# The third unit's MLP in one piece with seven products for its output, ahead of the last blocks of the first two units

## The chip, the cores and the metric

The kernel runs on one core of one Trainium2 chip. The metric is device time in microseconds (us) of a whole execution; before the change it is 658.83 us, the median of 3 runs (657.85 to 659.45).

A core has a matrix engine (TensorE, PE in the profile, with its weight loads listed apart as PEld), VectorE (DVE), ScalarE (ACT), GpSimd (POOL), and a queue (SP) that issues the transfers. Each works through its own list of instructions and waits for the others where it needs their results.

## The reference

A gated linear attention feeds an MLP. Sizes: 4 batches, 8 heads, 768 tokens, 48 channels per head; the MLP goes from 384 to 2048 and back.

```python
f = 1.0 / (1.0 + np.exp(-f_logit))
for t in range(S):
    state = f[:, :, t, :, None] * state + np.einsum('bhd,bhe->bhde', k[:, :, t], v[:, :, t])
    y[:, :, t] = np.einsum('bhd,bhde->bhe', q[:, :, t], state)
# (B,H,S,D) -> (B*S, H*D)
x = y.transpose(0, 2, 1, 3).reshape(B * S, H * D)
h = x @ w_in
g = h * (1.0 / (1.0 + np.exp(-1.702 * h)))
out = g @ w_out
```

Where the weights reach the kernel as 64-bit floats, it turns them into 32-bit ones itself ("conversions").

## The kernel before

The 3072 tokens are cut into 12 units of 256, numbered 0 to 11. A unit has an attention, written as a list of parts, and an MLP. The MLP of one unit fills TensorE while the attention of a later unit waits for the other engines. `merge` emits the parts of one unit's attention and, after each, a share of the list `fill`; each entry of the list has a width in columns, a function that emits it, and the number of converted weight pieces that it needs.

The MLP exists in two forms. For the first three units it is cut into four blocks of 4 x 128 hidden columns, as the weights arrive: `h` (48 products of 256 columns over the four blocks), then `o` with 32 products of 384 columns, summed up over the blocks in `sums`.

```python
def mlp_block(n, r):
    g, ffs = {}, range(r * FG, (r + 1) * FG)      # FG = 4, NGR = 4 blocks
    def done(tt, po):
        ...                                       # tile sums[n] at the first block
        acc = sums[n][:, tt]
        if r == 0:
            nc.scalar.copy(acc, po)
        else:
            nc.vector.tensor_tensor(acc, acc, po, ALU.add)
        if r == NGR - 1:
            store(n, tt, acc)
    return mlp_h(n, ffs, g), mlp_o(n, ffs, g, done)

def mlp_blocks(*blocks):                          # all h, then all o
    hs, os = zip(*(mlp_block(n, r) for n, r in blocks))
    return sum(hs, []) + sum(os, [])
```

From unit 3 on it is whole (`mlp_unit`), and `o` is made with seven products of half-sized matrices instead of eight: 56 products of 192 columns. These need sums of quarters of `w_out` (T, made once by `sums_of_b`) and sums of quarters of g (made per unit).

```python
def sums_of_b():
    for i in (1, 2, 3):
        T[i] = wp.tile(..., tag="bits", bufs=PAIRS_AHEAD)     # the place of the raw weights
    t4 = [wp.tile([P, DM], F32, tag="a", bufs=4) ...]
    for x in h: yield lambda x=x: sub(T[1][:, x], quarter(w_out, 0, 1, x), quarter(w_out, 0, 0, x))
    ...                                                       # T2, T3: two each; T4: four

def sums_of_a(n, g, b):
    j = b % 2
    if b < 2:
        g["S", j] = mlp.tile([P, FG, width(n)], F32, tag="g", bufs=6)
        tt(g["S", j][:, :, t1], g[j][:, :, t0], g[j][:, :, t1], ALU.subtract)
    else:
        tt(g[j][:, :, t1], g[j][:, :, t1], g[j + 2][:, :, t1], ALU.add)
        tt(g["S", j][:, :, t0], g[j][:, :, t1], g[j][:, :, t0], ALU.subtract)

def mlp_o7(n, g):
    ...
    products = (
        ("X", a(0, 0), b(0, 0), p1, True), ("W", a(1, 1), T_(4), p4, True), ("X", a(0, 1), b(1, 0), p2, False),
        ("Y", s(0), T_(2), p6, True), ("Z", a(1, 0), T_(1), p5, True), ("Y", s(1), T_(3), p7, False),
        ("Z", a(0, 1), b(1, 1), p3, False),
    )
    ...                                                       # 8 products of HC = 192 columns for each
    return [(HC, lambda p=p, f=f: one(*p, f), 0) for p in products for f in range(HF)]

def mlp_h(n, ffs, g, sums=False):
    def one(ff, c):
        if c == 0:
            if ff % FG == 0:
                g[ff // FG] = mlp.tile([P, FG, width(n)], F32, tag="g", bufs=6)
            t["ph"] = ps.tile([P, width(n)], F32, tag="mm", bufs=4)      # PSUM, shared with o
        nc.tensor.matmul(ph, lhsT=w_in[...], rhs=xTs[n][:, c, :], ...)
        if c == NK - 1:
            nc.scalar.activation(sg, ph, AF.Sigmoid, scale=1.702)
            nc.vector.tensor_tensor(g[ff // FG][:, ff % FG, :], ph, sg, ALU.mult)
            if sums and ff % FG == FG - 1:
                sums_of_a(n, g, ff // FG)
            ...
```

The conversions take five VectorE operations per piece of 128 x 384 (`chain`) and a copy on ScalarE; `convert()` emits one operation. The loop that mixes all this:

```python
def merge(n, fill, columns, share, pieces=0, hold=0, by=1.0, chores=()):
    parts = parts_of(n)
    ...
    for kind, fn in parts:
        ready = state["done"]                     # pieces converted so far
        fn()
        for chore in chores[:2]:
            chore()
        chores = chores[2:]
        at += share(kind)
        at_ops += converting.get(kind, 0)
        n_ops = min(int(pieces * NOP * at_ops / (by * total_ops)), pieces * NOP) - ops
        ...
        for i in range(n_ops):
            some(first + n_columns * i / n_ops)   # emit entries of fill up to this width
            convert()
        some(first + n_columns)
```

The parts of unit 3 are three score parts ("V"), a part that transposes the gates and queries of the next unit on VectorE, two that transpose keys on TensorE ("T"), one that transposes the next unit's keys on VectorE, and the state products ("S"). The calls:

```python
merge(0, fill, 0, steady, 8)
fill += mlp_blocks((0, 0)) + mlp_blocks((0, 1))
merge(1, fill, UNIT // 2 - LAG // 2, steady, 10, hold=1)
fill += mlp_blocks((1, 0), (1, 1)) + mlp_blocks((0, 2), (1, 2))
merge(2, fill, UNIT, steady, 8)
fill += mlp_blocks((2, 0), (2, 1)) + mlp_blocks((2, 2), (0, 3)) + mlp_blocks((1, 3), (2, 3))
merge(3, fill, 3 * UNIT // 2 - LAG // 2, steady, 6, by=0.7)
fill_order.close()                                # from here only TensorE keeps the program's order
for n in range(3, NALL):
    fill += mlp_unit(n)
for n in range(4, NALL):
    merge(n, fill, NFF * NK * U + 7 * HF * HC, steady, chores=list(sums_of_b()) if n == 4 else ())
for _, emit, _ in fill:
    emit()
```

Here LAG is 18 x 384 = 6,912 columns and UNIT is 24,576. Up to `fill_order.close()` every engine keeps the order in which the program emits; afterwards a scheduler orders the engines other than TensorE, and may place their instructions earlier.

Of the kernel before, what the change touches and what calls it, by code (L numbers as in the profile page):

```python
# [2 lines left out]

# [6 lines left out]
F32 = mybir.dt.float32  # L10
# [13 lines left out]
def kernel(  # L24
# [37 lines left out]
    P = 128  # L62
    C = 64
    G = 128
    U = 256
# [7 lines left out]
    NK = DM // P  # L73
    NFF = DFF // P
    FG = 4
    PAIRS_AHEAD = 3
    N_FILL = 3
# [9 lines left out]
    mlp = ctx.enter_context(tc.tile_pool(name="mlp", bufs=2))  # L87
# [52 lines left out]
    w_in = const.tile([P, NK, DFF], F32, name="w_in")  # L140
    w_out = const.tile([P, NFF, DM], F32, name="w_out")
# [4 lines left out]
    NGR = NFF // FG  # L146


    pieces, pairs = [], []
    for r in range(NGR):  # L150
        ffs = range(r * FG, (r + 1) * FG)
        for ff in ffs[::2]:
            f = slice(ff * P, (ff + 2) * P)
            pairs.append((w_in[:, :, f], [
                (lambda t: t[:D2], moe_w_in[0:NK * D2, f].rearrange("(c p) f -> p c f", c=NK)),
                (lambda t: t[D2:], moe_w_in[NK * D2:DM, f].rearrange("(c p) f -> p c f", c=NK)),
            ]))
        for ff in ffs[::2]:
            pairs.append((w_out[:, ff:ff + 2, :], [
                (lambda t: t[:], moe_w_out[ff * P:(ff + 2) * P, :].rearrange("(c p) f -> p c f", c=2))]))  # L160
        pieces += [w_in[:, :, ff * P:(ff + 1) * P] for ff in ffs] + [w_out[:, ff, :] for ff in ffs]
    NPC = 2 * FG
    NOP = 5
    fetched, todo = {}, []
    state = {"fetch": 0, "begin": 0, "done": 0}
# [21 lines left out]
    def begin_pair(m):  # L187

        chains = []
        for n in (2 * m, 2 * m + 1):
            if n not in fetched:
                continue
            dst = pieces[n]
            bits = fetched.pop(n)
            at = (slice(None),) * (len(dst.shape))
            lo, hi = bits[at + (0,)], bits[at + (1,)]

            def tmp(tag, bufs, n=n, dst=dst):  # L200
                t = wp.tile([P, DM], F32, tag=tag, name=f"{tag}_{n}", bufs=bufs)
                return t.rearrange("p (c f) -> p c f", c=NK) if len(dst.shape) == 3 else t[:]

            a = tmp("a", 4)
            nc.scalar.activation(a, hi.bitcast(F32), AF.Copy, scale=2.0 ** -112)
            chains.append(chain(dst, lo, hi, a, tmp))
        for ops in zip(*chains):  # L210
            todo.extend(ops)
        todo.append(None)
# [393 lines left out]
    HF, HC = NFF // 2, DM // 2  # L606
# [45 lines left out]
    def mlp_o7(n, g):  # L652
        a = lambda i, j: lambda f: g[j * 2 + f // FG][:, f % FG, i * G:(i + 1) * G]
        s = lambda i: lambda f: g["S", f // FG][:, f % FG, i * G:(i + 1) * G]
        b = lambda i, j: lambda f: quarter(w_out, i, j)[:, f]
        T_ = lambda i: lambda f: T[i][:, f] if i < 4 else T[4](f)
        t = {}

        def out_(tt):
            if "o" not in g:  # L660
                g["o"] = mlp.tile([P, U // P, DM], F32, tag="osb", name=f"osb_{n}", bufs=1)
            return g["o"][:, tt]

        def row(name):
            t[name] = mlp.tile([P, HC], F32, tag=name, name=f"{name}_{n}", bufs=1)
            return t[name]

        def p1():
            nc.scalar.copy(row("p1"), t["X"])

        def p4():
            nc.scalar.copy(row("p4"), t["W"])

        def p2():
            nc.scalar.copy(out_(0)[:, :HC], t["X"])
            last_sum(n, g)

        def p6():
            nc.vector.tensor_tensor(row("u2"), t["p1"], t["Y"], ALU.add)  # L679

        def p5():
            nc.scalar.copy(row("p5"), t["Z"])

        def p7():
            nc.vector.tensor_tensor(row("u3"), t["p1"], t["Y"], ALU.add)
            nc.vector.tensor_tensor(out_(1)[:, :HC], t["u3"], t["p4"], ALU.subtract)
            nc.vector.tensor_tensor(out_(1)[:, HC:], t["u3"], t["p5"], ALU.add)
            store(n, 1, out_(1))

        def p3():  # L690
            nc.vector.tensor_tensor(out_(0)[:, HC:], t["u2"], t["Z"], ALU.add)
            store(n, 0, out_(0))
# [8 lines that stand above are left out]
        def one(bank, lhs, rhs, done, new, f):  # L701
            if new and f == 0:
                t[bank] = ps.tile([P, HC], F32, tag="mm", name=f"o_{n}_{bank}", bufs=4)
            nc.tensor.matmul(  # L704
                t[bank], lhsT=lhs(f), rhs=rhs(f), start=(new and f == 0), stop=(f == HF - 1), skip_group_check=True,
            )
            if f == HF - 1:
                done()
        return [(HC, lambda p=p, f=f: one(*p, f), 0) for p in products for f in range(HF)]


    xTs = {}
# [1 line left out]
    def width(n):  # L714

        return U + (n == NALL - 1)

    def mlp_h(n, ffs, g, sums=False):
        t = {}

        def one(ff, c):
            if c == 0:
                if ff % FG == 0:
                    g[ff // FG] = mlp.tile([P, FG, width(n)], F32, tag="g", name=f"g_{n}_{ff}", bufs=6)
                t["ph"] = ps.tile([P, width(n)], F32, tag="mm", name=f"h_{n}_{ff}", bufs=4)
            ph = t["ph"]
            nc.tensor.matmul(  # L727
                ph, lhsT=w_in[:, c, ff * P:(ff + 1) * P], rhs=xTs[n][:, c, :], start=(c == 0), stop=(c == NK - 1)
            )
            if c == NK - 1:  # L730
                sg = mlp.tile([P, width(n)], F32, tag="sg", name=f"sg_{n}_{ff}")
                nc.scalar.activation(sg, ph, AF.Sigmoid, scale=1.702)  # L732
                nc.vector.tensor_tensor(g[ff // FG][:, ff % FG, :], ph, sg, ALU.mult)  # L733
                if sums and ff % FG == FG - 1:
                    sums_of_a(n, g, ff // FG)
                if width(n) > U:

                    by = g[ff // FG][:, ff % FG, U:]
                    if ff == 0:
                        g["last"] = mlp.tile([P, 1, DM], F32, tag="sum", name="sum_last", bufs=3)  # L740
                        nc.vector.tensor_scalar(g["last"][:, 0], w_out[:, 0, :], by, None, op0=ALU.mult)
                    else:
                        nc.vector.scalar_tensor_tensor(
                            g["last"][:, 0], w_out[:, ff, :], by, g["last"][:, 0], op0=ALU.mult, op1=ALU.add
                        )
        return [(NK * U, lambda ff=ff: [one(ff, c) for c in range(NK)], ff // FG * NPC + ff % FG + 1) for ff in ffs]
# [35 lines left out]
    def mlp_block(n, r):  # L782

        g, ffs = {}, range(r * FG, (r + 1) * FG)

        def done(tt, po):
            if r == 0 and tt == 0:
                sums[n] = mlp.tile([P, U // P, DM], F32, tag="sum", name=f"sum_{n}", bufs=3)
# [4 lines that stand above are left out]
                nc.vector.tensor_tensor(acc, acc, po, ALU.add)  # L793
            if r == NGR - 1:
                store(n, tt, acc)
        return mlp_h(n, ffs, g), mlp_o(n, ffs, g, done)

    def mlp_blocks(*blocks):

        hs, os = zip(*(mlp_block(n, r) for n, r in blocks))  # L800
        return sum(hs, []) + sum(os, [])


# [1 line left out]
    LAG = 18 * DM  # L805
# [28 lines left out]
            parts.append(("W", inter))  # L834
        return parts

    def merge(n, fill, columns, share, pieces=0, hold=0, by=1.0, chores=()):

# [6 lines left out]
        for kind, fn in parts:  # L847
            ready = state["done"]
            fn()
            for chore in chores[:2]:  # L850
                chore()
            chores = chores[2:]
            at += share(kind)
            at_ops += converting.get(kind, 0)
            n_ops = min(int(pieces * NOP * at_ops / (by * total_ops)), pieces * NOP) - ops
# [32 lines left out]
    fill = []  # L888
# [2 lines left out]
    merge(1, fill, UNIT // 2 - LAG // 2, steady, 10, hold=1)  # L891
    fill += mlp_blocks((1, 0), (1, 1)) + mlp_blocks((0, 2), (1, 2))
    merge(2, fill, UNIT, steady, 8)
    fill += mlp_blocks((2, 0), (2, 1)) + mlp_blocks((2, 2), (0, 3)) + mlp_blocks((1, 3), (2, 3))
    merge(3, fill, 3 * UNIT // 2 - LAG // 2, steady, 6, by=0.7)
    fill_order.close()
    for n in range(3, NALL):
        fill += mlp_unit(n)
    for n in range(4, NALL):
        merge(n, fill, NFF * NK * U + 7 * HF * HC, steady, chores=list(sums_of_b()) if n == 4 else ())  # L900
    for _, emit, _ in fill:
        emit()

# [28 lines left out]
```

## Time and profile before

| what | value |
|---|---|
| time | 658.83 us (657.85 to 659.45, 3 runs) |
| span of the profiled execution | 656.8 us |
| granted TensorE clock | 0.995 |
| TensorE on the chain that ended last | 84% of the span |
| VectorE on that chain | 9% |
| 12 units' hidden products (line 727) | 1152 instructions |
| three units' output in blocks (line 755) | 192 instructions |
| nine units' output in seven products (line 704) | 1008 instructions |

The busy shares are over the whole span. The core's first 140 us, in which the weights arrive and are converted, differ from the rest, so a stage is to be read by itself: the timeline of an engine lists its instructions in order, with the idle time ahead of one and what ended it in square brackets. A matmul's time as listed overlaps that of the next, so a pace is to be taken from the starts of long runs.

### The profile page before, as it was taken

The numbers are of one execution on the slowest core, as the hardware profiler recorded it, in microseconds if no ns is written. First come the engines' busy times: TensorE is split into PE (matmuls) and PEld (weight loads), VectorE is DVE, ScalarE is ACT, GpSimd is POOL, SyncE is SP. The second block draws the span as 40 slices with busy tenths as digits, with TensorE's granted clock in tenths as the row PEclk, the third lists the DMA queues.
The fourth block names the chain that finished last, engine by engine and source line by source line (L and its number), as shares of the span: only waits on it lengthen the run. The fifth ranks groups of instructions, "written<-read, shape, count | busy, mean of one in ns | idle before, by whom it ended". The sixth has DMA issues, their size and how long they took to land.

```text
span 656.8 us, 20370 instructions
## 1 busy us (share of the span) xinstructions
PE 630.0 (96%) x8946; PEld 541.2 (82%) x8946; DVE 444.7 (68%) x802; ACT 230.2 (35%) x477; POOL 53.4 (8%) x116
## 2 busy tenths in 40 slices
PE   6669999989999999999999999999999999999997
PEld 5546667766678689989989989989989989989997
DVE  2988887788887757657658658558558557553571
ACT  3464443243223423423324324324324324222120
POOL 3020020020001002002002002002002002000000
PEclk9998999999999999999999999999999999999999
DMA  8886975294125444524514515614603202101000
GB/s 190 222 201 164 225 180 133 75 225 78 43 60 151 135 106 117 143 52 118 148 45 121 148 44 120 160 31 119 166 26 104 67 25 62 40 2 26 25 1 24
DMA packets 67554, 67.67 MB, mean 103 GB/s; under 512 B 30410, under 2 KB 61290, under 8 KB 67466
## 3 DMA queue, kind: packets, MB, share of 16 engines
q1 hardware_dynamic: 67466, 66.38, 40.4%
q8 instruction: 70, 1.15, 0.8%
q14 instruction: 18, 0.15, 0.1%
HBM read 56.92 MB, written 8.65 MB: 100 GB/s over the span
## 4 chain that ended last, share of the span: by engine, by line
PE 84%; DVE 9%; ACT 2%; issue 2%; DMA 1%; SPq 0%; DVEq 0%; ACTq 0%
PE h L727 37%; PE o L755 7%; PE o_X L704 7%; PE o_Y L704 7%; PE o_Z L704 7%; PE sc L384 5%; PE y L448 4%; PE o_W L704 4%; PE t L339 2%; PE y L563 2%; PE sc L523 1%; PE tkn L505 1%; DVE X L439 1%; DMA xT<-yT 1%; DVE s L219 1%
## 5 line engine op out<-in xcount | busy, mean ns | idle before, releaser
L727 PE MATMUL h<-xT,w_in 128*128 128x256 f32 (+1 forms) x1152 | 260.4, 382 | 4.7 <-DMA xT<-yT 1.9
L727 PEld LDWEIGHTS h<-xT,w_in 128*128 128x128 f32 x1152 | 215.8, 190 | 38.7 <-issue 3.3
L733 DVE TENSOR_TENSOR g<-h,sg 128x256 f32<-128x256 f32 (+1 forms) x192 | 80.8, 422 | 99.4 <-ACT sg L732 97.0
L732 ACT ACTIVATE sg<-h 128x256 f32<-128x256 f32 (+1 forms) x192 | 73.4, 384 | 192.8 <-PE h L727 186.0
L423 ACT COPY Kc<-X 128x512 f32<-128x512 f32 x69 | 46.1, 668 | 120.4 <-DVE X L439 83.4
L755 PE MATMUL o<-w_out,g 128*128 128x384 f32 x192 | 66.4, 493 | 0.0
L439 DVE TENSOR_TENSOR X<-X,tot 128x1024 f32<-128x1024 f32 x45 | 55.2, 1226 | 15.4 <-PE sc L384 10.2
L755 PEld LDWEIGHTS o<-w_out,g 128*128 128x128 f32 x192 | 35.3, 190 | 22.8 <-issue 1.5
L704 PE MATMUL o_X<-w_out,g 128*128 128x192 f32 x288 | 51.9, 329 | 0.0
L704 PE MATMUL o_Y<-T,S 128*128 128x192 f32 x288 | 51.1, 331 | 0.1
L704 PEld LDWEIGHTS o_Y<-T,S 128*128 128x128 f32 x288 | 46.5, 190 | 2.6 <-DVE u L679 1.3
L704 PEld LDWEIGHTS o_X<-w_out,g 128*128 128x128 f32 x288 | 47.3, 190 | 0.9
L410 DVE TENSOR_TENSOR A<-sc,masks 128x512 f32<-128x512 f32 x72 | 46.7, 679 | 0.0
L448 PE MATMUL y<-A,vl 64*48 64x64 f32 x2304 | 41.3, 218 | 0.1
L448 PEld LDWEIGHTS y<-A,vl 64*48 64x48 f32 x2304 | 36.5, 121 | 3.5 <-issue 3.1
L376 POOL TENSOR_TENSOR tot<-F 128x512 f32<-128x512 f32 x12 | 12.5, 1040 | 327.9 <-DVE st L540 327.9
L327 DVE STREAM_TRANSPOSE X<-raw 128x1024 f32<-128x1024 f32 x18 | 36.7, 2039 | 2.4 <-PE y L563 2.4
L384 PE MATMUL sc<-X,Kc 48*64 48x64 f32 x1344 | 28.6, 222 | 8.5 <-DVE A L410 4.2
L384 PEld LDWEIGHTS sc<-X,Kc 48*64 48x64 f32 x1344 | 24.3, 136 | 15.1 <-ACT vl L288 6.0
L571 ACT COPY yT<-y 48x512 f32<-48x512 f32 x48 | 27.9, 580 | 13.9 <-PE y L563 13.3
L376 POOL TENSOR_TENSOR tot<-tot 128x256 f32<-128x256 f32 (+4 forms) x60 | 26.9, 448 | 4.7
L704 PE MATMUL o_Z<-w_out,g 128*128 128x192 f32 x144 | 26.6, 331 | 0.0
(91 smaller groups left out, 650.8 us busy)
## 6 DMA issues: line engine op xcount, KB each, us to landing
vl<-v_tok SPq DMA_DIRECT2D x60, 192.0 KB, 3.0
bits<-in_moe_w_out_dram SPq DMA_DIRECT2D x8, 768.0 KB, 9.7
bits<-in_moe_w_in_dram SPq DMA_DIRECT2D x8, 576.0 KB, 8.0
v_tok<-in_v_dram SPq DMA_DIRECT2D x10, 384.0 KB, 4.4
vn<-v_tok SPq DMA_DIRECT2D x10, 384.0 KB, 6.8
xT<-yT SPq DMA_DIRECT2D x24, 144.0 KB, 2.9
raw<-in_f_logit_dram SPq DMA_DIRECT2D x18, 192.0 KB, 4.2
raw<-in_q_dram SPq DMA_DIRECT2D x18, 192.0 KB, 3.7
```

The lines of the kernel that those rows point to most:

```text
L327: nc.vector.transpose(out.rearrange("p (a i j) -> p a j i", a=NP, j=R), raw[:, j].rearrange("p a (j d) -> p (a j) d", j=R)[:, :, :32],)
L376: nc.gpsimd.tensor_tensor(tn, t2[:, :, 0], t2[:, :, 1], ALU.mult)
L384: nc.tensor.matmul(out[g * HS:(g + 1) * HS, h, a, :], lhsT=lhs(h, a * U + g * G), rhs=rhs(h, a * U + g * G), start=True, stop=True,)
L410: nc.vector.tensor_tensor(A[:, :, c:c + w].rearrange("p h (x t) -> p h x t", t=64), t["sc"][:, :, c:c + w].rearrange("p h (x t) -> p h x t ...
L423: nc.scalar.copy(c.rearrange("p (n m) -> p n m", m=m), X[:, j, :NA].rearrange("p (n two m) -> p n two m", two=2, m=m)[:, :, hf, :],)
L439: nc.vector.tensor_tensor(qk, qk, by, ALU.mult)
L448: nc.tensor.matmul(dst(h, g, a), lhsT=vls[n, u][g * 64:(g + 1) * 64, (2 * a + h) * D:(2 * a + h + 1) * D], rhs=A(h, g, a), start=(start an ...
L704: nc.tensor.matmul(t[bank], lhsT=lhs(f), rhs=rhs(f), start=(new and f == 0), stop=(f == HF - 1), skip_group_check=True,)
L727: nc.tensor.matmul(ph, lhsT=w_in[:, c, ff * P:(ff + 1) * P], rhs=xTs[n][:, c, :], start=(c == 0), stop=(c == NK - 1))
L732: nc.scalar.activation(sg, ph, AF.Sigmoid, scale=1.702)
L733: nc.vector.tensor_tensor(g[ff // FG][:, ff % FG, :], ph, sg, ALU.mult)
L755: nc.tensor.matmul(t["po"], lhsT=g[ff // FG][:, ff % FG, tt * P:(tt + 1) * P], rhs=w_out[:, ff, :], start=(ff == ffs[0]), stop=(ff == ffs[ ...
```

## The change

The third unit (number 2) no longer goes in blocks. Its hidden part is made in one go, and its output with seven products, as in all later units. For that the sums T have to exist by then: they are emitted in the same stage, two after each part, as soon as all weights are converted, and the conversions are hurried (`by=0.35` in place of 0.7). The last blocks of units 0 and 1 go behind the first three quarters of unit 2's hidden part, and unit 2's last quarter behind those; two g tiles are taken for these blocks first, and the sums over unit 2's g are made all at once after its last hidden block. The seven products wait for all weights (`len(by_block)` is 32). What it is for: fewer columns through TensorE for one unit's output.

```diff
@@ mlp_o7
-        return [(HC, lambda p=p, f=f: one(*p, f), 0) for p in products for f in range(HF)]
+        return [(HC, lambda p=p, f=f: one(*p, f), len(by_block)) for p in products for f in range(HF)]
@@
+    def new_g(n, g, b):
+        g[b] = mlp.tile([P, FG, width(n)], F32, tag="g", name=f"g_{n}_{b}", bufs=6)
@@ mlp_h
-                if ff % FG == 0:
-                    g[ff // FG] = mlp.tile([P, FG, width(n)], F32, tag="g", name=f"g_{n}_{ff}", bufs=6)
+                if ff % FG == 0 and ff // FG not in g:
+                    new_g(n, g, ff // FG)
@@
                 if sums and ff % FG == FG - 1:
-                    sums_of_a(n, g, ff // FG)
+
+                    for b in range(NGR) if n < N_FILL and ff == NFF - 1 else [ff // FG] * (n >= N_FILL):
+                        sums_of_a(n, g, b)
@@ merge
-            for chore in chores[:2]:
-                chore()
-            chores = chores[2:]
+            if chores and state["done"] == len(by_block):
+                for chore in islice(chores, 2):
+                    chore()
@@ the calls
-    fill += mlp_blocks((2, 0), (2, 1)) + mlp_blocks((2, 2), (0, 3)) + mlp_blocks((1, 3), (2, 3))
-    merge(3, fill, 3 * UNIT // 2 - LAG // 2, steady, 6, by=0.7)
+
+    g2, ends = {}, [mlp_block(n, NGR - 1) for n in range(2)]
+    fill += [(0, lambda take=take: take(), 0) for _, _, take in ends]
+    fill += mlp_h(2, range(NFF - FG), g2, True) + sum((h + o for h, o, _ in ends), [])
+    fill += mlp_h(2, range(NFF - FG, NFF), g2, True) + mlp_o7(2, g2)
+    merge(3, fill, sum(w for w, _, _ in fill) - LAG, steady, 6, by=0.35, chores=sums_of_b())
     fill_order.close()
     for n in range(3, NALL):
         fill += mlp_unit(n)
     for n in range(4, NALL):
-        merge(n, fill, NFF * NK * U + 7 * HF * HC, steady, chores=list(sums_of_b()) if n == 4 else ())
+        merge(n, fill, NFF * NK * U + 7 * HF * HC, steady)
```

The rest of the diff renames a list (`pieces` to `by_block`) and lets `mlp_block` return a third item, the function that takes its g tile.

More of the change, by code (lines that the diff above doesn't have):

```diff
@@ L1 @@
 from contextlib import ExitStack
-from itertools import count
+from itertools import count, islice
 import concourse.bass as bass
@@ L146 @@
     NGR = NFF // FG
-    pieces, pairs = [], []
+    by_block, pairs = [], []
     for r in range(NGR):
@@ L160 @@
                 (lambda t: t[:], moe_w_out[ff * P:(ff + 2) * P, :].rearrange("(c p) f -> p c f", c=2))]))
-        pieces += [w_in[:, :, ff * P:(ff + 1) * P] for ff in ffs] + [w_out[:, ff, :] for ff in ffs]
+        by_block += [w_in[:, :, ff * P:(ff + 1) * P] for ff in ffs] + [w_out[:, ff, :] for ff in ffs]
     NPC = 2 * FG
@@ L194, in begin_pair @@
                 continue
-            dst = pieces[n]
+            dst = by_block[n]
             bits = fetched.pop(n)
@@ L795, in done @@
                 store(n, tt, acc)
-        return mlp_h(n, ffs, g), mlp_o(n, ffs, g, done)
+        return mlp_h(n, ffs, g), mlp_o(n, ffs, g, done), lambda: new_g(n, g, r)
     def mlp_blocks(*blocks):
-        hs, os = zip(*(mlp_block(n, r) for n, r in blocks))
+        hs, os, _ = zip(*(mlp_block(n, r) for n, r in blocks))
         return sum(hs, []) + sum(os, [])
@@ L835, in parts_of, with merge @@
         return parts
-    def merge(n, fill, columns, share, pieces=0, hold=0, by=1.0, chores=()):
+    def merge(n, fill, columns, share, pieces=0, hold=0, by=1.0, chores=None):
         parts = parts_of(n)
```

## The prediction

> **What bounds the kernel now.** I read the page's engine shares first, then the groups by line, then the engines' timelines for the stretch that the change rewrites, and the stretches of the whole span by busy time. The shares say TensorE:
>
> ```profile
> PE 630.0 (96%) x8946; PEld 541.2 (82%) x8946; DVE 444.7 (68%) x802; ACT 230.2 (35%) x477; POOL 53.4 (8%) x116
> ```
>
> The stretches say where it is not TensorE alone: between 300 and 640 us it is busy 20.00 of every 20.00 us (to within 0.05), while 120 to 140 has 18.68 and 140 to 160 has 17.55. So from about 213 us on, time is the sum of TensorE's work. The change touches the work of the third unit's MLP, which lies just before. (Units are numbered from 0 here as in the code: the third is unit 2.) In the timeline of TensorE I found that stretch by its score groups: three of them (144.5, 160.9, 174.0), two key transposes (191, 194.7) and the state products (201) are unit 3's attention, and the next unit's first product starts at 212.2. Lines of it:
>
> ```profile
> 150.84 2.83 PE L727 MATMUL h<-xT,w_in 128*128 128x256 f32 x12
> 154.61 2.96 PE L727 MATMUL h<-xT,w_in 128*128 128x256 f32 x12 [0.94 <-DVE sum L793]
> 158.08 2.86 PE L727 MATMUL h<-xT,w_in 128*128 128x256 f32 x12 [0.51 <-DVE g L733]
> 160.87 0.69 PE L384 MATMUL sc<-Qc,Kc 48*64 48x64 f32 x32
> ```
>
> Both idle times are VectorE's: a hidden block needs one of four PSUM buffers, and VectorE empties them late. VectorE at that moment:
>
> ```profile
> 152.27 1.28 DVE L410 TENSOR_TENSOR A<-sc,masks 128x512 f32<-128x512 f32 x2
> 153.47 0.62 DVE L226 TENSOR_SCALAR a<-s 128x384 int32<-128x384 int32 x2
> 154.01 0.55 DVE L793 TENSOR_TENSOR sum<-sum,o 128x384 f32<-128x384 f32 x1
> 154.47 1.02 DVE L227 SCALAR_TENSOR_TENSOR a<-bits,a 128x384 f32<-128x384 uint32 x2
> 155.41 0.55 DVE L793 TENSOR_TENSOR sum<-sum,o 128x384 f32<-128x384 f32 x1
> 155.87 1.82 DVE L622 TENSOR_TENSOR T<-w_out 128x768 f32<-128x768 f32 x2
> 157.61 0.41 DVE L733 TENSOR_TENSOR g<-h,sg 128x256 f32<-128x256 f32 x1
> ```
>
> Two readings. First, its order is the program's: conversions and sums alternate as the loop emits them. Second, the weights' sums T, which the source has one unit later (beside unit 4), already run here, at 155.9 and up to 195: once the fixed order of all engines ends, the scheduler pulls them forward. So "sums right behind the conversions" adds no VectorE time to this stretch; it only fixes places.
>
> The rows for the products:
>
> ```profile
> L755 PE MATMUL o<-w_out,g 128*128 128x384 f32 x192 | 66.4, 493 | 0.0
> L704 PE MATMUL o_X<-w_out,g 128*128 128x192 f32 x288 | 51.9, 329 | 0.0
> ```
>
> The means overlap one another, so I take paces from runs in the timelines. 16 instructions of 192 columns start at 600.31 and the next group at 602.91: 2.60 us, 0.1625 each. In the chain that ended last, 26 of 384 columns take 8.38 us: 0.322 each. 48 of a hidden block take 10.36 us: 0.216 each. Every product is two instructions (192 rows of L755 are 3 units x 32 x 2).
>
> [...] the sum at 154.01 sits behind two conversions though its product had ended by 150. [...] The sums over g measure 692, the 768-wide T 948 to 956; back to back they cost 0.61 and 0.87. [...]
>
> **The change part by part.**
> Removed and added on TensorE: unit 2's 32 products of 384 columns (64 instructions x 0.322 = 20.6 us) become 56 of 192 (112 x 0.1625 = 18.2 us): 2.4 us less. All else on TensorE is the same set, and from 213 us on every microsecond of it counts. VectorE gains for unit 2 six sums over g and two last sums (8 x 0.61 = 4.9) and five small output operations (5 x 0.35), and loses six sums of 0.46 (2.8): some 4 us more.
>
> Moved: I worked the merge loop's arithmetic through on paper; for before it gives the groups that the trace shows. Unit 3's stage gets 31,488 columns instead of 33,792 and leaves 6,912 over instead of 6,144. The 26 conversion operations still due fall into its first two parts (18 and 8) where three parts had 9, 9 and 8. The hidden blocks come first: 5 in part one, 9 in part two (7 of unit 2, 2 of unit 0); then unit 0's last block, unit 1's, and with the state products unit 2's last hidden block and the sums over g.
>
> Now a timetable with spacings from before's timelines (conversions 0.27 or 0.47, g 0.34, sum 0.46, promotion 1.14, transpose 1.88).
> Part one: VectorE is free of the masks at 153.5 as before. With the conversions emitted twice as densely the two sums end at 155.4 and 157.35 (before 154.5 and 155.9), the first g at 158.2 (before 157.9, behind the T that now are gone). TensorE ends five hidden blocks at 160.1; before it would have been 159.6. Loss 0.5 us.
> Part two: scores and level products to 162.1, four hidden blocks to 167.25. The next needs the sixth g. VectorE leaves part one at 162.95 and promotes twice with ScalarE's copies between (4.85 us in all, as from 162.17 to 167.02 before), then one conversion and that g: 168.6, with 0.14 to start 168.75. Loss 1.5 us. The rest runs through to 175.2.
> Part three: TensorE 2 us of attention, two hidden blocks of unit 0, its eight products, two hidden blocks of unit 1: to 187.55. VectorE has room: no loss. The products can begin before the last g (at 62.94 us before does so: a product follows its block at once, as it reads another slice).
> Next part: the raw gates and queries of unit 4 are transposed on VectorE, 2 x 1.88, then two T operations, 1.74, and only then come the g of unit 1's last two hidden blocks. VectorE begins at 188.4 behind the g before, so the first is there at 194.2. TensorE does those blocks (190.1), the first two products and a transpose (191.9), and then stands until 194.4. Loss 2.5 us. Before had all hidden blocks of two units ahead of the products there, so the same transposes at 189.78 delayed nothing.
> The rest: keys transposed at 200.9, promoted 205.2, g of unit 2 at 206.5 and 206.9, states to 209.6, last g 210.0, six sums to 213.6. TensorE starts X at 205.9, W at 208.5, and its last factor needs the g of 210.0 at 210.8: no wait. Y, the first to need the sums, comes after 215. TensorE ends the stage at 212.4.
> Before it ended at 212.2 with 768 columns less left over; at 1.69 ns (325/192) those are 1.3 us. Sum: +0.2 + 1.3 = +1.5 us. The other way: 0.5 + 1.5 + 2.5 - 2.4 = 2.1. I take +1.2, a little less than both, as waits laid out end to end tend to overstate: 658.8 + 1.2 = 660.0.
>
> **The rivals.** First, the gain arrives whole: VectorE keeps up, TensorE saves 2.4 and perhaps the 1.45 of idle shown above: 655 to 656.5. For it: VectorE has 9 to 26% free over the stretch (busy 17.36 of 19.00 us from 142, then 10.78 of 13.00 and 10.78 of 14.50), and T's 1.8 us no longer stand ahead of the first g. Against: parts one and two ask of VectorE what four parts did. Second, the late parts get worse: the scheduler puts a transpose of unit 5 among the sums over g, as it put one at 207.13 between g before; 2 us ahead of the last g would stop W for 1 to 2 us more: 662 to 663. Third, the last pair's conversion waits for its weights: issued at 140.6, median 9.7 us to land for that kind, needed at about 160: hidden, nothing lost. Fourth, a later stage loses cover because the leftover is larger: unlikely, as 6,912 columns are more, not less, work in hand when each unit begins.
>
> **Range and chances.** All effects lie within one stage of 70 us; saved work is certain, the three waits have an error of about 1 us each. 656.5 to 663.0 should hold it 8 times in 10. Two per cent are 13 us, more than any of these: 0.01 faster, 0.98 within, 0.01 slower.
>
> **What would show it.** In the changed timeline: L704 with 112 instructions more, L755 with 64 less. Of my three waits: a hidden block late in the second part waiting for g; in the stretch of unit 1's last products one wait of about 2.5 us on g, with two transposes and two T on VectorE before it; the two early sums some 1 to 1.5 us later. Unit 4's first state product on TensorE near 212.4. Wrong would be: no idle there of over 1 us (then 656), or idle within X, W, Y for the sums (then 662 or more), or new idle after 220.

## The result and the profile after

The changed kernel takes 666.61 us (median of 4 executions, 664.32 to 667.56) beside 658.34 us for the kernel before on the same chip: a ratio of 1.0122, 95% interval 1.0088 to 1.0156. Run once more, in a session with 59 executions of the kernel before, it took 665.60 beside 659.47: 1.0073 (1.0048 to 1.0097). So it is 6 to 8 us slower in the medians, where I had forecast 1.2 us slower and at most 663.0.

TensorE's work did not grow: 112 instructions of 192 columns stand for 64 of 384. The page of the changed kernel, engines and two groups of line 704:

```profile
PE 631.4 (95%) x8994; PEld 550.2 (83%) x8994; DVE 446.9 (67%) x809; ACT 229.2 (34%) x479; POOL 60.0 (9%) x116
...
L704 PE MATMUL o_Y<-T,S 128*128 128x192 f32 x320 | 57.6, 329 | 2.9 <-DVE u L679 2.9
L704 PE MATMUL o_X<-w_out,g 128*128 128x192 f32 x320 | 59.6, 331 | 0.0
```

The span grew by 8.0 us, TensorE's busy time by only 1.4: most of the rest is idle time. The second row names a wait that was not in my list: 2.9 us ahead of products into Y, for VectorE's line 679. TensorE's timeline has all of it. Columns: start, duration, instructions; in brackets the idle time before and what ended it.

```profile
157.62 1.56 PE L730 MATMUL h<-xT,w_in 128*128 128x256 f32 x6 [1.74 <-DVE sum L798]
159.55 2.86 PE L730 MATMUL h<-xT,w_in 128*128 128x256 f32 x12 [0.37 <-DVE sum L798]
...
164.33 5.45 PE L730 MATMUL h<-xT,w_in 128*128 128x256 f32 x24
170.75 6.74 PE L730 MATMUL h<-xT,w_in 128*128 128x256 f32 x30 [0.97 <-DVE g L736]
...
193.53 0.81 PE L760 MATMUL o<-w_out,g 128*128 128x384 f32 x2
196.76 3.70 PE L760 MATMUL o<-w_out,g 128*128 128x384 f32 x6 [2.42 <-DVE g L736]
200.29 0.60 PE L505 MATMUL tkn<-ident,X 128*128 128x128 f32 x4
...
222.58 2.76 PE L704 MATMUL o_Z<-T,g 128*128 128x192 f32 x16
228.20 2.22 PE L704 MATMUL o_Y<-T,S 128*128 128x192 f32 x12 [2.85 <-DVE u L679]
```

VectorE's list ahead of the two g that ended the wait of 2.42 us holds the two transposes and the two operations of T that the prediction put there:

```profile
190.81 2.03 DVE L327 STREAM_TRANSPOSE F<-raw 128x1024 f32<-128x1024 f32 x1
192.69 2.03 DVE L327 STREAM_TRANSPOSE X<-raw 128x1024 f32<-128x1024 f32 x1
194.55 1.81 DVE L622 TENSOR_TENSOR T<-w_out,T 128x768 f32<-128x768 f32 x2
196.27 0.76 DVE L736 TENSOR_TENSOR g<-h,sg 128x256 f32<-128x256 f32 x2
```

Against before's paces the start-to-start distances lose: in the first score part 2.8 us (before 2.3), in the second 1.2 (before 0.0), in unit 1's last products 2.6, then 1.6 more because the six instructions from 196.76 take 3.53 us where six take 1.94, and 3.0 in unit 4. That is 9.0 us more than before. The seven products give back 2.4, and the later units run 1.3 us shorter (422.6 us from unit 3's first hidden block at 235.69 to the last group at 658.30, before 423.9). Sum +5.3. Measured from the stage's first product with the states (line 563) to the start of the last product group: 144.11 to 658.30 = 514.2, before 142.03 to 650.70 = 508.7: +5.5. The four lines, before's two first:

```profile
142.03 0.32 PE L563 MATMUL y<-X,st 48*48 48x64 f32 x4 [0.20 <-DVE st L543]
650.70 2.76 PE L704 MATMUL o_Z<-w_out,g 128*128 128x192 f32 x16
144.11 0.32 PE L563 MATMUL y<-X,st 48*48 48x64 f32 x4 [0.19 <-DVE st L543]
658.30 2.76 PE L704 MATMUL o_Z<-w_out,g 128*128 128x192 f32 x16
```

I call this distance **the stretch**; it leaves out the start, which varies (below).

The slow six: in the stretches by busy time, the third number from the end of a line, ahead of the DMA share and GB/s, is the granted TensorE clock. It had fallen behind the wait of 2.42 us, and had not around that of 2.85:

```profile
196.00:201.00 5.00, 4.24 (x11) 2.62 (x12) 4.03 (x8) 0.07 (x1) 0.61 (x2) 0.66 0.90 200
219.00:230.00 11.00, 8.15 (x51) 7.85 (x50) 9.00 (x13) 5.83 (x11) 1.25 (x2) 1.00 0.28 70
```

Now VectorE between the last hidden block of unit 2 and line 679, which reads Y:

```profile
214.12 2.11 DVE L641 TENSOR_TENSOR S<-g 128x512 f32<-128x512 f32 x2
216.15 0.88 DVE L643 TENSOR_TENSOR g<-g,g 128x512 f32<-128x512 f32 x1
216.96 2.07 DVE L327 STREAM_TRANSPOSE F<-raw 128x1024 f32<-128x1024 f32 x1
...
221.38 2.03 DVE L327 STREAM_TRANSPOSE X<-raw 128x1024 f32<-128x1024 f32 x1
223.26 0.34 DVE L540 TENSOR_TENSOR st<-st,tot 128x192 f32<-128x192 f32 x1
223.52 1.22 DVE L439 TENSOR_TENSOR X<-X,tot 128x1024 f32<-128x1024 f32 x1
...
227.80 0.35 DVE L679 TENSOR_TENSOR u<-p,o_Y 128x192 f32<-128x192 f32 x1
```

It is busy for 14 us with no gap over 0.13 us: six sums, two transposes of unit 5 that the scheduler placed among them, the last sums, unit 4's promotions (line 439, which multiplies X by gate totals). The first product into Y ended on TensorE at about 222.6; the second product into Y adds to the same PSUM tile, called a bank in the code. The second started at 228.20, right behind VectorE's read of the first result (line 679, 0.35 us from 227.80).

### The profile page after: what moved, and what is told of

Same layout as the page of the kernel before. It is cut to its first block, busy times and chain, and to the rows that moved or that the text cites. A ratio compares the mean times of both kernels' runs of the same rounds, so it can differ in the third digit from the quotient of the medians.

```text
span 664.8 us, 20470 instructions
## 1 busy us (share of the span) xinstructions
PE 631.4 (95%) x8994; PEld 550.2 (83%) x8994; DVE 446.9 (67%) x809; ACT 229.2 (34%) x479; POOL 60.0 (9%) x116
## 4 chain that ended last, share of the span: by engine, by line
PE 80%; DVE 13%; issue 2%; ACT 2%; DMA 2%; SPq 1%; DVEq 0%; ACTq 0%
PE h L730 34%; PE o_Y L704 8%; PE o_X L704 7%; PE o_Z L704 7%; PE sc L384 5%; PE y L448 4%; PE o L760 4%; PE o_W L704 4%; PE y L563 2%; DVE X L327 1%; DVE X L439 1%; PE tkn L505 1%; PE sc L523 1%; PE t L339 1%; DVE s L219 1%
## 5 line engine op out<-in xcount | busy, mean ns | idle before, releaser
L704 PE MATMUL o_Y<-T,S 128*128 128x192 f32 x320 | 57.6, 329 | 2.9 <-DVE u L679 2.9
L704 PE MATMUL o_X<-w_out,g 128*128 128x192 f32 x320 | 59.6, 331 | 0.0
L704 PEld LDWEIGHTS o_Y<-T,S 128*128 128x128 f32 x320 | 52.2, 190 | 4.4 <-DVE u L679 3.1
L704 PEld LDWEIGHTS o_X<-w_out,g 128*128 128x128 f32 x320 | 52.4, 190 | 1.5
L760 PE MATMUL o<-w_out,g 128*128 128x384 f32 x128 | 46.7, 508 | 2.4 <-DVE g L736 2.4
L760 PEld LDWEIGHTS o<-w_out,g 128*128 128x128 f32 x128 | 24.0, 196 | 18.4 <-DVE g L736 3.4
L357 POOL COPY q_last<-X 128x4 f32<-128x4 f32 x12 | 13.1, 1095 | 162.0 <-DVE X L327 104.1
L704 PE MATMUL o_W<-T,g 128*128 128x192 f32 x160 | 27.6, 326 | 0.0
```

The source lines that it names most:

```text
L704: nc.tensor.matmul(t[bank], lhsT=lhs(f), rhs=rhs(f), start=(new and f == 0), stop=(f == HF - 1), skip_group_check=True,)
L760: nc.tensor.matmul(t["po"], lhsT=g[ff // FG][:, ff % FG, tt * P:(tt + 1) * P], rhs=w_out[:, ff, :], start=(ff == ffs[0]), stop=(ff == ffs[ ...
```

## The experiments

In each, the theory was that the loss is TensorE waiting for VectorE's order, in several separate waits. "Stretch" is as above, from the profile of that run, with 508.7 for before and 514.2 for the change.

**Hidden blocks of the last two blocks first.**

```diff
-    fill += mlp_h(2, range(NFF - FG), g2, True) + sum((h + o for h, o, _ in ends), [])
+    fill += mlp_h(2, range(NFF - FG), g2, True) + sum((h for h, _, _ in ends), []) + sum((o for _, o, _ in ends), [])
```

> The changed kernel with one edit: the hidden blocks of units 0 and 1 both ahead of their products. Theory (the loss is TensorE waiting for VectorE's order, four waits in all): the wait of 2.4 us in unit 1's last products goes, and with it the low TensorE clock of about 3 us behind it (1.6 us): 666.6 - 4 = 662.5. Rival (the loss comes from the start, where instructions arrived 2 us later, or from the larger leftover): nothing moves, 666.

Measured: 662.05 us beside 658.97 (1.0040, 1.0025 to 1.0056); stretch 511.7. The 2.4 us wait and the slow clock behind it are gone (granted clock 1.00 in 190 to 200 and in 196 to 201). The wait in unit 4 stayed, and this time the slow clock followed that one (0.84 in 219 to 230; 12 instructions in 3.77 us, at pace 1.95), which is why the stretch is 2.5 us shorter and not the 4 that were expected:

```profile
192.84 2.75 PE L760 MATMUL o<-w_out,g 128*128 128x384 f32 x8
...
223.42 3.84 PE L704 MATMUL o_Y<-T,S 128*128 128x192 f32 x12 [2.94 <-DVE u L679]
```

**Conversions spread as before** (`by=0.35` back to `by=0.7`).

> The changed kernel with by=0.7 again: conversions spread as before, the sums T and the products of the last blocks come later. Theory: the losses in the first two score parts (0.6 and 1.2 us) go back to before's 0.8 or so; as the products of unit 0 then are held until the transposes are out, the 2.4 us wait with its slow clock may go too: 660.5 to 664.5. The wait of 3 us in unit 4 stays. Rival (waits do not matter): 666.

Measured: 662.30 us (1.0034, 1.0022 to 1.0047); stretch 510.5. The first two parts lose 0.33 us in listed waits for VectorE (and 0.48 for a transfer of xT), and the 2.4 us wait is gone; but unit 0's products now wait 1.58 us for the last converted `w_out`, W waits 1.07 us for T4, and Y 2.36 us in unit 4. Later conversions moved part of the loss instead of removing it.

**Four of unit 2's six sums earlier.**

```diff
-                if sums and ff % FG == FG - 1:
-                    for b in range(NGR) if n < N_FILL and ff == NFF - 1 else [ff // FG] * (n >= N_FILL):
-                        sums_of_a(n, g, b)
+                if sums and n < N_FILL:
+                    for b in {NFF - FG: (0, 1, 2), NFF - 1: (3,)}.get(ff, ()):
+                        sums_of_a(n, g, b)
+                elif sums and ff % FG == FG - 1:
+                    sums_of_a(n, g, ff // FG)
```

> The changed kernel with four of unit 2's six sums over g moved ahead, behind the 13th hidden block. Theory: the six sums in a row are what holds up the first output operation of Y in unit 4 (2.85 us of wait); 2.4 us of them gone leaves 0.5 to 1 us: 664.3. Rival (the scheduler's transposes of unit 5 hold it up): the wait stays above 2 us, 666.

Measured: 665.59 us (1.0084, 1.0064 to 1.0104); stretch 512.3. The wait on Y fell to 0.50 us, so the six sums do feed it. But W now waits twice for g, 0.73 us each, as the sums stand ahead of those g; and 1.6 of the 1.9 us gained against the change is the slow clock, which did not follow the 2.41 us wait in this execution (granted clock 1.00 in 196 to 201). The sums moved a wait.

**The program's order kept through unit 4** (`fill_order.close()` after unit 4's stage).

> The changed kernel with the program's order kept on all engines for one unit more (unit 4's stage), so that the scheduler puts no transposes of unit 5 among unit 2's sums. Theory of the transposes: the 2.85 us wait in unit 4 falls to under 0.5 us: 663.7. Rival (the sums alone do it): it stays at 1.5 to 3 us: 665 to 666.6.

Measured: 667.03 us (1.0107, 1.0074 to 1.0140); stretch 516.1, the longest of all. The wait in unit 4 fell to 0.27 us as expected of the transposes. It came back one unit later, where VectorE was behind in turn, again with slow products behind it: 12 in 3.70 us from start to start, 2.14 in unit 4 (and 0.70 us on g ahead of it, at 249.10):

```profile
221.30 2.22 PE L704 MATMUL o_Y<-T,S 128*128 128x192 f32 x12 [0.27 <-DVE u L679]
...
274.18 3.77 PE L704 MATMUL o_Y<-T,S 128*128 128x192 f32 x12 [2.43 <-DVE u L679]
```

So it takes both, the sums and the transposes: either one moved away, the wait on Y falls to half a microsecond or less in that place (0.50 and 0.27 us), and something else waits. What they act through is the wait itself, so I took that away:

**A bank of its own for the second Y.** The second output is then added to the first one's sum, `u2`, in SBUF.

```diff
-            ("Y", s(0), T_(2), p6, True), ("Z", a(1, 0), T_(1), p5, True), ("Y", s(1), T_(3), p7, False),
+            ("Y", s(0), T_(2), p6, True), ("Z", a(1, 0), T_(1), p5, True), ("Y", s(1), T_(3), p7, True),
@@ p7
-            nc.vector.tensor_tensor(row("u3"), t["p1"], t["Y"], ALU.add)
+            nc.vector.tensor_tensor(row("u3"), t["u2"], t["Y"], ALU.add)
```

> The changed kernel with a PSUM bank of its own for the second product into Y, so that it need not wait until VectorE has read the first. Theory (the unit 4 wait is that read, late in VectorE's list): the wait of 2.85 us on it goes and one on ScalarE's copy of X's bank, some 2 us earlier, takes its place: 1 us of wait left, 664.5. Rival (the bank is not what is waited for): 2.85 us as before, 666.6.

Measured: 661.74 us beside 659.55 (1.0039, 1.0024 to 1.0054); stretch 510.0. Of the 4.2 us less in the stretch 1.6 are the slow clock, which did not follow the 2.41 us wait, ahead of the edit's place, in this execution (granted clock 1.00 in 190 to 200 and in 196 to 201). No wait at all was left there: I had expected one on X's bank, but the product started at 221.42 while ScalarE copied X's result only at 222.17, so it did not wait for that copy. VectorE's line 679 still came at 224.05, late as before:

```profile
218.82 2.76 PE L704 MATMUL o_Z<-T,g 128*128 128x192 f32 x16
221.42 2.11 PE L704 MATMUL o_Y<-T,S 128*128 128x192 f32 x12
```

```profile
224.05 0.35 DVE L679 TENSOR_TENSOR u<-p,o_Y 128x192 f32<-128x192 f32 x1
```

**Hidden blocks first, and conversions spread** (the first two edits together).

> The changed kernel with both edits: hidden blocks of units 0 and 1 first, and conversions spread as before (by=0.7). Theory: no loss in the two first score parts beyond before's, none at the last blocks' products; left are some 1 us on T4 and 2.4 to 3 us in unit 4: 660 to 661. Rival (the two edits remove the same wait, so they do not add up): 662.

Measured: 662.13 us (1.0033, 1.0017 to 1.0048); stretch 510.7. The waits are the expected ones (1.14 us on T4, 2.35 on Y, and the 12 products behind the latter took 3.38 us from start to start, at pace 1.95), yet the time is that of either edit alone, as the rival had it: each of the two had removed the 2.4 us wait by itself, and spreading the conversions pays for its other gain at T4.

**All four edits.**

> All four edits together: hidden blocks first, conversions spread, sums split, own bank for the second Y. Theory: every wait that I found is gone or under 1 us, so the saved 2.4 us shows: 656.5 to 658, at or under the kernel before (658.9). Rival (the shift of work leaves VectorE behind somewhere else): 660 or more.

Measured: 660.72 us (1.0018, 1.0003 to 1.0033); stretch 510.6. The rival held: with T late and four sums moved ahead of it, W waits 0.79 us for g and then 2.59 us for T4 (1.14 without the moved sums), and the products behind that wait ran slow again (the 8 into X from 214.86 took 2.70 us from start to start, 1.39 in the change):

```profile
209.02 1.57 PE L704 MATMUL o_W<-T,g 128*128 128x192 f32 x8 [0.79 <-DVE g L736]
213.18 1.89 PE L704 MATMUL o_W<-T,g 128*128 128x192 f32 x8 [2.59 <-DVE T L622]
```

**The kernel before with more left over** (unit 3's stage emits 2,304 columns less).

> The kernel before with one edit: unit 3's stage emits 2,304 columns less, so that more is left over for each later stage. In before each later unit waits some 0.2 us ahead of the second product into Y; in the changed kernel, with a larger leftover, it doesn't. Theory (the place of the products decides): those waits go, 657.5. Rival: no difference, 658.9.

Measured: 660.34 us beside 659.55 (1.0019, 1.0000 to 1.0038); stretch 508.7, as before. The profile has the expected gain in the later units and loses it in unit 3's stage: from that stage's start to unit 4's first product it saves 2.6 us where 2,304 columns at 1.69 ns are 3.9. So it gains nothing.

**The change once more.**

> The changed kernel once more, unaltered. Its first profile began unit 3's stage at 144.1 us, 2 us later than before's, in a stretch where both run the same instructions. Theory (the start varies from execution to execution and is no part of the change): this profile begins it anywhere from 141.3 to 145.8, and the waits of 1.74, 0.97, 2.4 and 2.85 us stand again; the median may come down to 664 to 665. Rival (the change delays the start): 144 again, 666.6.

Measured: 665.60 us (1.0073, 1.0048 to 1.0097). The stage began at 142.6 this time, with the waits 1.69, 0.97, 2.42 and 2.85 us and the slow six again; stretch 514.2, the same to 0.1. The first profile's later start was not the change.

**Hidden blocks first, own bank; and the same with conversions spread a little (`by=0.45`).**

> The changed kernel with two edits: hidden blocks of units 0 and 1 first, and a bank of its own for the second Y. Theory: the two longest waits go (2.4 and 2.85 us) with the slow clock that may follow them, the losses of the first two score parts stay (2 us): from the stage's start to the last products 507 us, 1.6 less than before's 508.7; 657.5 to 659. Rival (some other wait comes in): 661 or more.

> As the run before it, and the conversions spread a little (by=0.45: 14 and 12 operations in the first two parts in place of 18 and 8). Theory: the waits of 1.74 and 0.97 us shrink by half, nothing later is held up: another 0.5 to 1 us less, 656.5 to 658.5. Rival: the waits only move from the first part to the second: no difference.

Measured: the first 658.65 us beside 659.47 (0.9980, 0.9965 to 0.9995), stretch 507.3; the second 657.65 us (0.9958, 0.9943 to 0.9972), stretch 505.8. Both are faster than the kernel before, the first by no more than the disagreement left open in the next experiment, the second by 1.8 us in the medians and 2.8 in the profile. Of its waits between the stage's first scores and the end, all that is listed:

```profile
154.88 1.56 PE L730 MATMUL h<-xT,w_in 128*128 128x256 f32 x6 [1.35 <-DVE sum L798]
156.75 2.86 PE L730 MATMUL h<-xT,w_in 128*128 128x256 f32 x12 [0.31 <-DVE sum L798]
220.19 0.69 PE L384 MATMUL sc<-X,Kc 48*64 48x64 f32 x32 [0.20 <-ACT Kc L423]
```

The wait of the second part (0.97 us) is gone and the first is a little shorter: with 14 and 12 conversions, all weights are still done before the third part, so T is not late.

**The kernel before with the own bank.**

> The kernel before with a bank of its own for the second Y in all nine units. It tells what the bank alone gives, without the change. Theory: before's waits of 0.2 us in each later unit go: 1.4 us less, 657.5 beside 658.9. Rival: no difference that can be measured.

Measured: 660.07 us (1.0003, 0.9989 to 1.0017), no difference, though the stretch of its one profile is 1.3 us shorter (507.4). The bank alone is thus not what makes the last version faster: against this kernel, which has the bank too, that version is 2.4 us shorter in the medians (657.65 beside 660.07) and 1.5 in the stretch. Why its profile and its medians disagree by a microsecond is open.

## Why the prediction was wrong

**What held.** The saving on TensorE (2.4 us), that the rest is VectorE's order, and the wait in unit 1's last products: forecast 2.5 us, from the transposes and T ahead of two g; measured 2.42, and gone with the hidden blocks first. The losses of the first two parts, forecast 0.5 and 1.5 us, were 0.6 and 1.2. T did not add VectorE time to the stage (busy for 57.01 us of it before, 56.59 after). Up to the end of unit 2's last g the timetable held: forecast 210.0, measured 214.1, which less the later start (2.1) and the slow six (1.6) is 210.4.

**The step that failed** is the one that ended the timetable at 212.4 us: "Y, the first to need the sums, comes after 215", from which nothing was to be lost behind that point. I looked at what Y reads and not at what the second product into Y overwrites. It adds to a bank that VectorE has yet to read, and VectorE had 14 us of sums, transposes and promotions in one row in its list. It cost 3.0 us; "new idle after 220", which the prediction gave as a sign of being wrong, is this wait. The six sums behind that last g, forecast to take 3.6 us, took 6.7 with a transpose among them. The second rival came near it (a transpose of unit 5 did fall among the sums) but named W as the victim, and W did not wait. The own bank shows the cause: VectorE as late as before, and no wait.

**The second omission** is the pace of the products behind a wait: six instructions at 0.59 us each in place of 0.32, 1.6 us, at a granted clock of 0.66. I had counted each wait at its bare length. It is no fixed cost: in three experiments the same wait had no slow clock behind it (1.00 granted in 190 to 200 and in 196 to 201 of each).

These two make 4.6 us. With them, and with the 1.3 us that the later units gained and that I had not counted either, my first sum of +1.5 becomes 4.8; the stretch measured 5.5. Unit 4's first state product came at 216.6 from a start 2.1 us later, so at 214.5 on before's clock in place of 212.4: the slow six are 1.6 of that. The rest up to 8.3 us in the first medians I put down to the start and the spread of executions, which no run separates: the second session gave 6.1.

**The shading** from 1.5 and 2.1 to 1.2, because "waits laid out end to end tend to overstate", had no support in the trace and went the wrong way.

**The fourth rival**, a later stage that loses cover by the larger leftover, did not come, as I had thought: the later units ran 1.3 us shorter.

## What to carry to other kernels

When work moves to where another engine is already behind, follow each accumulation to its next writer: here the second product into Y, which adds to a bank that VectorE still had to read, waited 2.85 us for that read behind 14 us of other work in VectorE's list. A bank of its own took the wait away (2.85 us to none), while reordering the list only moved it (to W, to T4, or to the next unit). Order fills so that everything whose result passes through the busy engine comes well ahead of its use: hidden blocks ahead of all products took away a wait of 2.4 us here. A saving of 2.4 us on the bounding engine showed only when the two longest of these waits were gone and no new one had come in: the change as made cost 6 to 8 us, with three small edits it gains 1.8.

## What the runs showed of the hardware that I had not expected

From unit 3's stage on, half of the 14 profiles have a stretch of some 3 us in which TensorE's instructions take longer, mostly behind a wait. In three of them the granted clock was read over that time, and was lower: 0.66 in 196 to 201 of the first profile of the change and 0.77 in the second, both behind the 2.42 us wait, and 0.84 in 219 to 230 with the hidden blocks first. It did not follow the waits of 2.41, 2.42 and 2.41 us in the same place in three of the experiments (1.00 in 190 to 200 and in 196 to 201), and elsewhere slow products followed waits of 2.35, 2.43, 2.59 and 2.94 us but not those of 2.36 and 2.85. In two profiles they came with no listed wait above 0.5 us in the 8 us ahead of them, at the start of unit 3's stage: 16 products of 384 columns took 6.45 us from start to start with the order kept and 6.62 in the kernel before with the own bank, 5.28 in the kernel before. Lines of the first:

```profile
144.20 1.10 PE L384 MATMUL sc<-X,Kc 48*64 48x64 f32 x32
145.23 6.62 PE L760 MATMUL o<-w_out,g 128*128 128x384 f32 x16
```

There it cost nothing: the first score part took 18.25 us from the stage's start, 18.23 in the change, because the waits for VectorE behind it shrank from 2.11 to 0.75 us. What decides when TensorE slows down is not shown: waits of the same length had it and had it not.

The same instructions reach unit 3's stage between 141.3 and 146.6 us in the 14 profiles, early idle times without a visible releaser among the differences (3.37 us at 43.9 in the first profile of the change, at most 1.05 in before). Single executions of one kernel spread by 5 us and more (657.40 to 663.08 in 63 of the kernel before) for that reason or others that I did not separate, so effects of 1 to 2 us were read from the stretch.
